# Local and global attention with a gated MLP on one core: a new order table, wishes for engines, displaced TensorE operations, and another conversion of the float64 weights

## The chip, the cores and the metric

The kernel runs on one core of a Trainium2 chip. The metric is the device time of one execution in microseconds (us). Engines are named as in the profile: PE (TensorE; PEld is its weight load), DVE (VectorE), ACT (ScalarE), POOL (GpSimd), SP (SyncE, which issues the DMAs).

## What is computed

```python
# attention: B, H, S, D = 4, 8, 768, 64; n_global 8, n_local 96
scores = q @ k.T / sqrt(D) + bias        # bias: slope of the head times distance
scores = where(is_global | is_local, scores, -1e9)
a = exp(scores - max); a = a / (sum(a) + 1e-9)
x = (a @ v) as (B, 768, 512)
# gated MLP: w_in (512, 1024) and w_out (512, 512) are float64, w_sg (768, 768) is float32
h = gelu(x @ w_in); u, v = h[..., :512], h[..., 512:]
v_n = (v - mean(v)) / sqrt(var(v) + 1e-6) * g_ln
v_s = einsum('ts,bsd->btd', w_sg, v_n) + b_sg
out = x + (u * v_s) @ w_out
```

## The kernel before

**Attention.** There are 48 units: four batches, three stretches of 256 queries, four pairs of heads. A unit is two DMAs (qk, v); `score`, PE products of 64x64 quarters of the array (`s_ps`, L886); `softmax`, in which DVE adds the bias and takes the row minimum (L918), ACT takes the exponential (L923), a small operation adds 1e-9 to the sums (L930 ACT, L932 POOL, L934 DVE), DVE takes the reciprocal (L936) and one of ACT (L943), POOL (L945) or DVE (L948) scales the rows; `turn`, which turns the weights over, by PE transposes (L1007) and copies (L1012, L1013) for the first 16 units and by DVE transposes (L974) and a DMA through memory later; `weigh`, the quarter products with v (`av`, L1035); and `take`, which puts the result into x as a high and a low part (`xh` L1132 or L1133, high L1144 or L1146, low L1150). A run of quarter products between products of the full array is called a block below.

**MLP.** Every product is three PE matmuls (L539, L540, L541: high by high and the two mixed ones). The tiles are V (`mm_ps<-win,x`, 512 columns, with gelu L558 to L563 and the layer norm: statistics L597 to L599 on DVE, a power on POOL L602, the normalising L604 on DVE, and the split in high L573 and low L577), U (`mm_ps<-x,win`, 384 columns), the mix over the sequence (`mm_ps<-wsg,z`, L631, L634 and a split) and the output (`mm_ps<-gt,wout`, L662, L665, DMA L668).

**Weights.** `load_split` brings 20 float64 pieces (16 of 256 columns, 4 of 512: `win` and `wout`) as pairs of int32 words. ACT scales the upper word (L704); three DVE passes, a shift (L707) and two with two inputs (L709, L711), put the lost bits in; then a high part (L714 ACT, L715 DVE) and a low part (L716) are split off. The pieces of `wsg` need the split only.

**What sets the order.** `Plan` records 2566 operations, each with one or more ways (an engine and an estimate of its cost). `due` gives every operation a due time from the order of the PE operations; `search` adds to it a shift from the table `SHIFTS` (one digit for each operation, in steps of 0.05 us) as its `key`; `order` goes through the engines and picks, among the operations that are ready, the one with the lowest key and the way that would end first; `emit` chains the instructions of an engine in that order. In the first 75 us `keep_on` (L483 to L489) puts matmuls with zeros (`<-on`, "fillers" below) ahead of a PE operation where the plan has PE idle. In the start the first 12 units, the pieces of `win` and the first V tiles are worked off together; the first U tile follows after 20 V and attention steps, then the mix tiles, and the first output tile at about 86 us.

## Time and profile before

| what | value |
|---|---|
| median of three runs | 410.22 us (410.19 to 410.34) |
| span of the profiled execution | 410.0 us |
| PE busy | 398.2 us (97%) |
| DVE busy | 322.0 us (79%) |
| ACT busy | 216.7 us (53%) |
| POOL busy | 183.6 us (45%) |
| clock of PE, 12 to 30 us | 0.92 |

The span is the time from the first to the last instruction of the one execution that the hardware profiler recorded; no separate time is given for that execution. An engine that is busy for nearly all of a stretch can set the pace there; what an engine waited for is told by its row in the view of waits. Matmuls are pipelined, so the time between two starts, not the duration of one, is what a matmul costs.

### The profile page before, as it was taken

What the parts mean: (1) busy time and instruction counts of PE and PEld (TensorE: products, weight loads), DVE (VectorE), ACT (ScalarE), POOL (GpSimd) and SP (SyncE); (2) the same over time, 40 slices, a digit from 0 to 9 for tenths busy, and PEclk for the clock granted to TensorE, in tenths of its full rate; (3) what the DMA queues carried; (4) which work ended last, traced back from release to release, by engine and by line L of the source; (5) the groups of instructions that cost most, each with busy time, mean ns of one, the idle gap of its engine ahead of it and who ended that gap; (6) DMA issues with size and microseconds to landing.
All of it is one profiled execution on the core that took longest, in us unless ns stands there. A gap on an engine that the chain in (4) does not pass through costs nothing.

```text
span 410.0 us, 12434 instructions
## 1 busy us (share of the span) xinstructions
PE 398.2 (97%) x4593; PEld 362.0 (88%) x4593; DVE 322.0 (79%) x1088; ACT 216.7 (53%) x726; POOL 183.6 (45%) x332
## 2 busy tenths in 40 slices
PE   7999999999999999999999999999999999999993
PEld 4768778898998989899999888999999889999993
DVE  7998999999978999877677899867677668663552
ACT  5999999875646856535432666551432325310110
POOL 3324553373548675666446454563446242303100
PEclk9899999999999999999999999999999999999998
DMA  7874765237786896646888673652856410001002
GB/s 232 283 228 121 218 199 160 81 106 234 229 237 213 264 289 197 174 148 200 254 228 248 217 235 96 203 153 96 245 186 203 148 39 21 0 2 70 10 1 83
DMA packets 50035, 67.14 MB, mean 164 GB/s; under 512 B 5808, under 2 KB 33968, under 8 KB 49968
## 3 DMA queue, kind: packets, MB, share of 16 engines
q1 hardware_dynamic: 49968, 66.28, 52.7%
q8 instruction: 38, 0.62, 0.6%
q14 instruction: 29, 0.24, 0.2%
HBM read 47.91 MB, written 18.35 MB: 162 GB/s over the span
## 4 chain that ended last, share of the span: by engine, by line
PE 85%; DVE 9%; ACT 1%; issue 1%; POOL 0%; DVEq 0%; POOLq 0%
PE mm_ps L539 24%; PE mm_ps L541 23%; PE mm_ps L540 23%; PE av L1035 7%; PE s_ps L886 6%; PE tps L1007 2%; DVE p L918 1%; DVE stage L711 1%; DVE stage L709 1%; DVE st L597 1%; DVE win L716 1%; DVE vg L563 1%; DVE stage L707 0%; DVE p L948 0%; DVE vg L560 0%
## 5 line engine op out<-in xcount | busy, mean ns | idle before, releaser
L923 ACT ACTIVATE p<-p,pst 128x168 f32<-128x168 f32 (+1 forms) x192 | 80.9, 424 | 28.8 <-DVE pst L918 23.7
L945 POOL TENSOR_SCALAR p<-p,pst 128x168 f32<-128x168 f32 (+1 forms) x137 | 56.8, 430 | 27.5 <-DVE pst L936 27.0
L539 PE MATMUL mm_ps<-wsg,z 128*128 128x384 f32 x192 | 65.0, 339 | 0.0
L541 PE MATMUL mm_ps<-wsg,z 128*128 128x384 f32 x192 | 64.3, 335 | 0.1
L540 PE MATMUL mm_ps<-wsg,z 128*128 128x384 f32 x192 | 64.2, 334 | 0.0
L918 DVE CUSTOM_DVE_ANT_0 p<-s_ps,bias 128x168 f32<-128x168 f32 (+1 forms) x192 | 53.5, 319 | 6.5 <-PE s_ps L886 4.9
L665 POOL TENSOR_TENSOR o<-o,x 128x384 f32<-128x384 f32 x28 | 28.6, 1021 | 52.5 <-DVE o L662 39.0
L1035 PE MATMUL av<-pt,v 64*64 64x128 f32 (+1 forms) x1408 | 48.8, 252 | 1.0 <-DVE pt L1013 0.7
L1035 PEld LDWEIGHTS av<-pt,v 64*64 64x64 f32 x1408 | 37.4, 134 | 9.9 <-issue 5.3
L539 PE MATMUL mm_ps<-x,win 128*128 128x384 f32 x128 | 43.9, 343 | 0.0
L539 PE MATMUL mm_ps<-gt,wout 128*128 128x384 f32 x128 | 43.0, 336 | 0.0
L540 PE MATMUL mm_ps<-gt,wout 128*128 128x384 f32 x128 | 43.0, 336 | 0.0
L541 PE MATMUL mm_ps<-gt,wout 128*128 128x384 f32 x128 | 42.9, 335 | 0.0
L541 PE MATMUL mm_ps<-x,win 128*128 128x384 f32 x128 | 42.8, 335 | 0.0
L540 PE MATMUL mm_ps<-x,win 128*128 128x384 f32 x128 | 42.8, 334 | 0.0
L558 ACT ACTIVATE u<-mm_ps 128x384 f32<-128x384 f32 x32 | 15.6, 488 | 45.7 <-PE mm_ps L541 45.0
L886 PE MATMUL s_ps<-qk 64*64 64x64 f32 (+2 forms) x1408 | 39.5, 242 | 0.1
L539 PE MATMUL mm_ps<-win,x 128*128 128x512 f32 x96 | 39.5, 411 | 0.0
L886 PEld LDWEIGHTS s_ps<-qk 64*64 64x64 f32 x1408 | 34.2, 135 | 4.1 <-issue 2.7
L541 PE MATMUL mm_ps<-win,x 128*128 128x512 f32 x96 | 37.7, 393 | 0.0
L540 PE MATMUL mm_ps<-win,x 128*128 128x512 f32 x96 | 37.7, 392 | 0.0
L539 PEld LDWEIGHTS mm_ps<-wsg,z 128*128 128x128 f32 x192 | 36.0, 188 | 1.4 <-issue 0.9
(112 smaller groups left out, 902.1 us busy)
## 6 DMA issues: line engine op xcount, KB each, us to landing
qk<-in_qk_in_dram SPq DMA_DIRECT2D x32, 328.0 KB, 3.8
pt<-far SPq DMA_DIRECT2D x24, 384.0 KB, 4.9
v<-in_v_in_dram SPq DMA_DIRECT2D x32, 256.0 KB, 4.1
out_dram<-o SPq DMA_DIRECT2D x32, 192.0 KB, 3.4
far<-tt SPq DMA_DIRECT2D x48, 96.0 KB, 1.9
far<-stage SPq DMA_DIRECT2D x48, 96.0 KB, 2.4
qk<-in_qk_in_dram SPq DMA_DIRECT2D x16, 276.0 KB, 3.6
v<-in_v_in_dram SPq DMA_DIRECT2D x16, 192.0 KB, 4.2
```

The lines of the kernel that those rows point to most:

```text
L539: mm(ps.ap, ah, bh, start=(i == 0), stop=False)
L540: mm(ps.ap, ah, bl, start=False, stop=False)
L541: mm(ps.ap, al, bh, start=False, stop=(i == n - 1))
L558: op([on_act(n) + (lambda: nc.scalar.activation(out.ap, h.ap, AF.Square, scale=math.sqrt(GELU_C * GELU_A)),)], [h], [out])
L563: op([on_dve(n) + (lambda: nc.vector.scalar_tensor_tensor(out.ap, out.ap, 1.0, h.ap, ALU.add, ALU.mult),)], [h], [out])
L665: lo = lambda eng: eng.tensor_tensor(o.ap, o.ap, xm[:, 1, :].bitcast(F32), ALU.add)
L886: nc.tensor.matmul(s_ps[h][e * HQ:(e + 1) * HQ, i * W + c0:i * W + c0 + n], qk[rows, qc:qc + HQ], qk[rows, QW + k0:QW + k0 + n], start=Tru ...
L918: nc.vector.tensor_tensor_reduce(out=p[:, g, cols], in0=s_ps[h][:, i * W:i * W + nk], in1=bias[:, 2 * j + h, w0:w0 + nk], op0=ALU.add, op1 ...
L923: op([on_act(nk, 0.225) + (lambda p=p, g=g, cols=cols, i=i: nc.scalar.activation(p[:, g, cols], p[:, g, cols], AF.Exp, bias=st[:, 0, i, g: ...
L945: op([on_pool_ts(nk, -0.10) + (partial(scaled, lambda o, a, c: nc.gpsimd.tensor_scalar(o, a, c, 1.0, ALU.mult, ALU.mult)),), on_act(nk, 0. ...
L1007: nc.tensor.transpose(tps[:, a * P:(a + 1) * P], pc[:, c:c + P], ident)
L1035: nc.tensor.matmul(to, v[rows, vc:vc + D], of, stop=True, skip_group_check=True, **kw)
```

## The change

There is a new `SHIFTS` table, whose digits now run over the whole range. For a PE operation a digit no longer shifts its due time: it displaces the operation by so many places in the list of PE operations. A second table, `WAYS`, has a letter for each operation: A, D or P allow only the way on ACT, DVE or POOL, a dash allows all. POOL is added as a way for the high parts (`split`, `load_split`, `take`) and the bias, ACT and POOL as ways of the normalising; for this POOL makes two small operations instead of one after the statistics (`power`). In the conversion of float64 the passes L707, L709 and L711 give way to a copy of one 16-bit quarter beside another (`beside`, on POOL or DVE), a DVE shift with a mask on the upper words, and one DVE pass with two inputs.

```diff
--- before.py
+++ after.py
@@ -11,6 +11,7 @@
 F32 = mybir.dt.float32
 F32R = mybir.dt.float32r
 BF16 = mybir.dt.bfloat16
+I16 = mybir.dt.int16
 I32 = mybir.dt.int32
 AF = mybir.ActivationFunctionType
 ALU = mybir.AluOpType
@@ -58,30 +59,57 @@
 DIGITS = "0123456789ABCDEFGHIJKLMNOPQRSTUVWXYZabcdefghijklmnopqrstuvwxyz-"
 
 SHIFTS = (
-    "VdcVXYiVeZpLWbTXPWjkIXjPCbojUQ-XVe7ZLXXrICVYZVKMNTFBePnQ8WNYfaeuV2PlWAhAQRISUVFT3qSMPPWYPLUvdWapCJTaXfAYUTgl"
...
+    "XHB003VbY000E5QRmULOkerH3KLhj-nH8w8d5z6L70v5P50Z5nt2x99CbT62UGEO7nA-p7cCGM0pttPmt-00gfuL3JHH5T0K20bCPcGL039W"
...
+)
+
+WAYS = (
+    "------A------------ADD--PD---------D-ADDP-DD--A-A--------P--PAP---DA----DD--A-A-----------P-P--P--------D--D"
...
 )
 
 TURNS = 16
@@ -278,9 +306,12 @@
             for other in o.before:
                 other.after.append(o)
             o.left = len(o.before)
-            if o.quarters is not None:
-                t += self.switch(mode, o.quarters)
-                o.due, t, mode = t, t + o.ways[0][1], o.quarters
+        pe = [o for o in self.ops if o.quarters is not None]
+        places = {o: i + o.moved for i, o in enumerate(pe)}
+        self.pe = sorted(pe, key=places.get)
+        for o in pe:
+            t += self.switch(mode, o.quarters)
+            o.due, t, mode = t, t + o.ways[0][1], o.quarters
         later = {}
         for kind, bufs in kinds.items():
             for b, next_b in zip(bufs, bufs[self.places[kind]:]):
@@ -298,8 +329,8 @@
 
     def search(self, start):
 
-        for o, digit in zip(self.ops, SHIFTS, strict=True):
-            o.key = o.due + (DIGITS.index(digit) - 31) * 0.05
+        for o in self.ops:
+            o.key = o.due + (0.0 if o.quarters is not None else o.moved * 0.05)
         done, end = self.order(start, RULES)
         assert end < math.inf, "no op can go on"
         return done
@@ -341,7 +372,7 @@
-        pe = [o for o in self.ops if o.quarters is not None]
+        pe = self.pe
...
-            for w in o.ways:
+            for w in o.open:
                 wait[w[0]].append(o)
...
@@ -493,6 +524,9 @@
         bb = nc.cur_bb.bb
         why, sync = (mybir.DependencyInfo(c, mybir.DependencyReason.DATA)
                      for c in (mybir.DependencyClass.NoSync, mybir.DependencyClass.Sync))
+        for o, digit, way in zip(self.ops, SHIFTS, WAYS, strict=True):
+            o.moved = DIGITS.index(digit) - 31
+            o.open = [w for w in o.ways if w[0][0] == way] or o.ways
         self.due()
         for o in self.search(start):
             n = len(bb.instructions)
@@ -573,7 +607,8 @@
             put(out[:, 0, :], src.ap)
 
         op([on_act(n, 0.03) + (partial(high, nc.scalar.copy),),
-            on_dve_ts(n / 2) + (partial(high, nc.vector.tensor_copy),)], [src], [(out, 0)])
+            on_dve_ts(n / 2) + (partial(high, nc.vector.tensor_copy),),
+            on_pool_ts(n) + (partial(high, nc.gpsimd.tensor_copy),)], [src], [(out, 0)])
         lo = lambda eng: eng.tensor_tensor(out[:, 1, :], src.ap, out[:, 0, :].bitcast(F32),
                                            ALU.subtract)
         op([on_dve_sb(n) + (lambda: lo(nc.vector),), on_pool(n) + (lambda: lo(nc.gpsimd),)],
@@ -599,10 +634,18 @@
             nc.vector.tensor_scalar(rs[:, 0:1], mv[:, 1:2], 4e-6, None, ALU.add)
 
         op([on_dve(FF, 0.40) + (stats,)], [g], [st, mv, rs])
-        op([("POOL_TS", 0.55, 0.6, lambda: nc.gpsimd.tensor_tensor(
-            rs[:, 1:2], rs[:, 0:1], w.mhalf, ALU.pow))], [], [rs])
+
+        def power():
+            nc.gpsimd.tensor_tensor(rs[:, 1:2], rs[:, 0:1], w.mhalf, ALU.pow)
+            nc.gpsimd.tensor_scalar(rs[:, 0:1], mv[:, 0:1], rs[:, 1:2], -1.0, ALU.mult, ALU.mult)
+
+        op([("POOL_TS", 0.80, 0.85, power)], [mv], [rs])
         op([on_dve_ts(FF, -0.14) + (lambda: nc.vector.tensor_scalar(
-            g.ap, g.ap, mv[:, 0:1], rs[:, 1:2], ALU.subtract, ALU.mult),)], [mv, rs], [g])
+            g.ap, g.ap, mv[:, 0:1], rs[:, 1:2], ALU.subtract, ALU.mult),),
+            on_act(FF, 0.05) + (lambda: nc.scalar.activation(
+                g.ap, g.ap, AF.Identity, bias=rs[:, 0:1], scale=rs[:, 1:2]),),
+            on_pool_ts(FF) + (lambda: nc.gpsimd.tensor_scalar(
+                g.ap, g.ap, mv[:, 0:1], rs[:, 1:2], ALU.subtract, ALU.mult),)], [mv, rs], [g])
         z = self.z[t] = Buf(lambda i: self.zp.tile([P, 2, FF], F32R, tag=f"z{i}", name="z"), "z")
         self.split(g, z, FF)
 
@@ -704,15 +747,19 @@
         op([on_act(n, 0.07) + (lambda: nc.scalar.mul(
             f.ap, words()[:, :, 1].bitcast(F32), 2.0 ** -112),)], [raw], [f])
 
-        op([("DVE_TS", 0.07 + n / 1850, 0.15 + n / 1850, lambda: nc.vector.tensor_scalar(
-            a(), a(), 3, None, ALU.logical_shift_left))], [], [f])
+        def beside(put):
+            of = raw.ap.bitcast(I16).rearrange("p (n w) -> p n w", w=4)
+            put(of[:, :, 2], of[:, :, 1])
+
+        op([on_pool_ts(n) + (partial(beside, nc.gpsimd.tensor_copy),),
+            on_dve_ts(n) + (partial(beside, nc.vector.tensor_copy),)], [f], [raw])
+        op([on_dve_ts(n) + (lambda: nc.vector.tensor_scalar(
+            words()[:, :, 1], words()[:, :, 1], 13, -0x7ffffff9, ALU.arith_shift_right, ALU.bitwise_and),)], [], [raw])
         op([on_dve_sb(n, 0.02) + (lambda: nc.vector.scalar_tensor_tensor(
-            a(), words()[:, :, 0], 29, a(), ALU.logical_shift_right, ALU.bitwise_or),)], [raw], [f])
-        op([on_dve_sb(n, 0.02) + (lambda: nc.vector.scalar_tensor_tensor(
-            a(), words()[:, :, 1], -0x80000000, a(), ALU.bitwise_and, ALU.bitwise_or),)],
-           [raw], [f])
+            a(), a(), 3, words()[:, :, 1], ALU.logical_shift_left, ALU.bitwise_or),)], [raw], [f])
     op([on_act(n, 0.03) + (lambda: nc.scalar.copy(t[:, 0, k, cols], f.ap),),
-        on_dve_ts(n / 2) + (lambda: nc.vector.tensor_copy(t[:, 0, k, cols], f.ap),)], [f], [(t, part)])
+        on_dve_ts(n / 2) + (lambda: nc.vector.tensor_copy(t[:, 0, k, cols], f.ap),),
+        on_pool_ts(n) + (lambda: nc.gpsimd.tensor_copy(t[:, 0, k, cols], f.ap),)], [f], [(t, part)])
     lo = lambda eng: eng.tensor_tensor(t[:, 1, k, cols], f.ap, t[:, 0, k, cols].bitcast(F32),
                                        ALU.subtract)
     op([on_pool(n) + (lambda: lo(nc.gpsimd),), on_dve_sb(n) + (lambda: lo(nc.vector),)],
@@ -856,7 +903,9 @@
                 op([("DVE_TS", 0.065 + n / 3300, 0.145 + n / 3300, lambda h=h, cols=cols: nc.vector.tensor_scalar(
                     bias[:, h, cols], dist[:, cols], -(2.0 ** (2 - h)), None, ALU.mult)),
                     on_act(n) + (lambda h=h, cols=cols: nc.scalar.mul(
-                        bias[:, h, cols], dist[:, cols], -(2.0 ** (2 - h))),)],
+                        bias[:, h, cols], dist[:, cols], -(2.0 ** (2 - h))),),
+                    on_pool_ts(n) + (lambda h=h, cols=cols: nc.gpsimd.tensor_scalar(
+                        bias[:, h, cols], dist[:, cols], -(2.0 ** (2 - h)), 1.0, ALU.mult, ALU.mult),)],
                    [(dist_b, part) for part in parts], [(bias_b, (h, part)) for part in parts])
 
     def wire(words):
@@ -1144,6 +1193,8 @@
             op([on_act(t1 - t0, 0.03) + (lambda x=x, cols=cols, src=src: nc.scalar.copy(
                 x[:, 0, cols], half[:, src]),),
                 on_dve_ts((t1 - t0) / 2) + (lambda x=x, cols=cols, src=src: nc.vector.tensor_copy(
+                    x[:, 0, cols], half[:, src]),),
+                on_pool_ts(t1 - t0) + (lambda x=x, cols=cols, src=src: nc.gpsimd.tensor_copy(
                     x[:, 0, cols], half[:, src]),)], [half], ts)
 
             def low(eng, x=x, cols=cols, src=src):
```

Counted over the program, PE has 41 blocks of quarter products instead of 45, all its other products unchanged in number, and 83 fillers instead of 57. The scaling of rows stands on DVE in 53 operations (19 before), on ACT in 56 (36) and on POOL in 83 (137); of the 24 normalisings 9 are on DVE, 10 on ACT and 5 on POOL; of the 20 copies `beside`, 13 are on DVE (3 of them of 512 columns) and 7 on POOL. Ahead of the first U tile stand 20 quarter products more than before, in 18 blocks (19 before); between the first U and the first output tile there are 2 blocks (5), and behind it 21 (21).

PE at the first U tile (`av` are products with v, `s_ps` scores, `on` fillers), before:

```order
L541 MATMUL mm_ps<-win,x 128x512
L1035 MATMUL av<-pt,v 64x128 x4
L1035 MATMUL av<-pt,v 64x64 x4
L539 MATMUL mm_ps<-x,win 128x384
L540 MATMUL mm_ps<-x,win 128x384
```

And after the change, where eleven more pairs like the last two rows stand before the first U product:

```order
L575 MATMUL mm_ps<-win,x 128x512
L1084 MATMUL av<-pt,v 64x128 x4
L1084 MATMUL av<-pt,v 64x64 x4
L935 MATMUL s_ps<-qk 64x104 x4
L935 MATMUL s_ps<-qk 64x64 x4
L935 MATMUL s_ps<-qk 64x104 x4
L935 MATMUL s_ps<-qk 64x64 x4
L1084 MATMUL av<-pt,v 64x128 x4
L519 LDWEIGHTS on
L519 MATMUL mm_ps<-on 128x384
```

A score and part of a further product with v have moved ahead of the first U tile, and twelve fillers of 384 columns stand there where there were none.

DVE at the conversions of the last pieces of `win` ahead of the first U tile, before:

```order
L709 SCALAR_TENSOR_TENSOR stage<-stage 128x256
L707 TENSOR_SCALAR stage<-stage 128x256
L711 SCALAR_TENSOR_TENSOR stage<-stage 128x256 x3
L709 SCALAR_TENSOR_TENSOR stage<-stage 128x256
L716 TENSOR_TENSOR win<-stage,win 128x256
L711 SCALAR_TENSOR_TENSOR stage<-stage 128x256
L716 TENSOR_TENSOR win<-stage,win 128x256
L715 CAST win<-stage 128x256
```

And after:

```order
L756 TENSOR_SCALAR stage<-stage 128x256
L758 SCALAR_TENSOR_TENSOR stage<-stage 128x256 x2
L756 TENSOR_SCALAR stage<-stage 128x256 x2
L758 SCALAR_TENSOR_TENSOR stage<-stage 128x256 x2
L763 TENSOR_TENSOR win<-stage,win 128x256 x4
L763 TENSOR_TENSOR wsg<-stage,wsg 128x384
```

Each piece has two passes here in place of three, and the copies `beside` stand further ahead; four low parts of `win` follow one another.

POOL at the first V tiles, before:

```order
L945 TENSOR_SCALAR p<-p,pst 128x168
L602 TENSOR_TENSOR rs<-rs,small 128x1
L1150 TENSOR_TENSOR x<-xh,x 128x128 x2
L945 TENSOR_SCALAR p<-p,pst 128x168
L577 TENSOR_TENSOR z<-vg,z 128x512
L932 TENSOR_SCALAR pst<-pst 128x4
```

And after:

```order
L607 CAST z<-vg 128x512
L994 TENSOR_SCALAR p<-p,pst 128x168
L612 TENSOR_TENSOR z<-vg,z 128x512
L639 TENSOR_TENSOR rs<-rs,small 128x1
L640 TENSOR_SCALAR rs<-mv,rs 128x1
L647 TENSOR_SCALAR vg<-vg,mv,rs 128x512
L607 CAST z<-vg 128x512
L612 TENSOR_TENSOR z<-vg,z 128x512
```

POOL now has high parts and a normalising of 512 columns among its work, and the second small operation behind the power.

## Rows read from the trace of the kernel before

**Rows 1.** The page: the span, and the busy time of each engine.

```profile
span 410.0 us, 12434 instructions
PE 398.2 (97%) x4593; PEld 362.0 (88%) x4593; DVE 322.0 (79%) x1088; ACT 216.7 (53%) x726; POOL 183.6 (45%) x332
```

**Rows 2.** Windows: length, then PE, PEld, DVE, ACT, POOL busy, PE clock, DMA share, GB/s.

```profile
12.00:30.00 18.00, 17.21 (x323) 13.15 (x317) 17.83 (x70) 17.41 (x68) 6.14 (x11) 0.92 0.75 248
30.00:60.00 30.00, 29.25 (x568) 22.71 (x568) 27.50 (x128) 29.57 (x110) 15.30 (x31) 1.00 0.62 190
60.00:86.00 26.00, 25.43 (x229) 22.37 (x229) 25.69 (x84) 23.32 (x76) 10.76 (x15) 1.00 0.39 114
86.00:403.50 317.50, 317.40 (x3365) 298.49 (x3363) 241.42 (x761) 138.63 (x449) 147.60 (x249) 1.00 0.52 159
```

**Rows 3.** PE's waits from 62 to 404 us: total, times, longest.

```profile
PE tps L1007 <- DVE vg L563: 0.5, 1, 0.5
```

**Rows 4.** Timeline at the first U tile: start, duration, engine, operation.

```profile
66.34 0.67 PE L1035 MATMUL av<-pt,v 64*64 64x128 f32 x16
66.51 0.83 DVE L716 TENSOR_TENSOR win<-stage,win 128x256 fp32r<-128x256 f32 x2
66.69 0.80 POOL L945 TENSOR_SCALAR p<-p,pst 128x128 f32<-128x128 f32 x1
66.94 0.44 PE L539 MATMUL mm_ps<-x,win 128*128 128x384 f32 x1
```

**Rows 5.** Timeline of PE: a switch inside a block, then a block between full products.

```profile
304.35 1.08 PE L1035 MATMUL av<-pt,v 64*64 64x128 f32 x48
305.25 0.77 PE L886 MATMUL s_ps<-qk 64*64 64x104 f32 x32
...
315.51 0.33 PE L540 MATMUL mm_ps<-wsg,z 128*128 128x384 f32 x1
315.69 0.34 PE L541 MATMUL mm_ps<-wsg,z 128*128 128x384 f32 x1
315.96 1.13 PE L1035 MATMUL av<-pt,v 64*64 64x128 f32 x48
317.02 0.50 PE L539 MATMUL mm_ps<-win,x 128*128 128x512 f32 x1
317.36 0.40 PE L540 MATMUL mm_ps<-win,x 128*128 128x512 f32 x1
317.59 0.39 PE L541 MATMUL mm_ps<-win,x 128*128 128x512 f32 x1
```

**Rows 6.** DVE groups by form, float64 passes: count, busy us, mean ns, idle before.

```profile
L709 DVE SCALAR_TENSOR_TENSOR stage<-stage 128x256 int32<-128x256 int32 x16 | 6.9, 431 | 0.2
L707 DVE TENSOR_SCALAR stage<-stage 128x256 int32<-128x256 int32 x16 | 4.9, 305 | 0.0
...
L709 DVE SCALAR_TENSOR_TENSOR stage<-stage 128x512 int32<-128x512 int32 x4 | 2.8, 693 | 0.1
...
L707 DVE TENSOR_SCALAR stage<-stage 128x512 int32<-128x512 int32 x4 | 1.7, 436 | 0.0
```

**Rows 7.** DVE groups by form, of kinds that change engine.

```profile
L604 DVE TENSOR_SCALAR vg<-vg,mv,rs 128x512 f32<-128x512 f32 x24 | 12.9, 541 | 1.8 <-POOL rs L602 1.6
...
L948 DVE TENSOR_SCALAR p<-p,pst 128x168 f32<-128x168 f32 x16 | 6.0, 398 | 0.1
...
L1133 DVE COPY xh<-av 128x128 f32<-128x128 f32 x11 | 3.1, 277 | 0.0
...
L716 DVE TENSOR_TENSOR win<-stage,win 128x512 fp32r<-128x512 f32 x4 | 2.7, 681 | 0.0
...
L1150 DVE TENSOR_TENSOR x<-xh,x 128x256 fp32r<-128x256 f32 x4 | 1.7, 414 | 0.0
```

**Rows 8.** Scaling on DVE: duration in ns least/median/longest, first and last start, forms.

```profile
L948 DVE TENSOR_SCALAR p<-p,pst x19: 277/341/1076, 9.0 to 133.2; 128x168 f32<-128x168 f32 x16, 128x128 f32<-128x128 f32 x3
```

**Rows 9.** The same of scaling on POOL.

```profile
L945 POOL TENSOR_SCALAR p<-p,pst x137: 361/405/811, 9.0 to 312.6; 128x168 f32<-128x168 f32 x111, 128x128 f32<-128x128 f32 x26
```

More of the change, by code (lines that the diff above doesn't have):

```diff
@@ new lines @@
+    "kQVEMxTUafgesQvKso9Fcqm-u8xN-m-2A0lCv--0m-Sxu0W7Jjf8CXTHjz6g-ZXX5YHbh8E2FEjL1HsS3BSRuaAnzWx-yN-H835Prbsd6HMQ"
+    "8FYComk9Xd-E0p01h2M-O5czBMTXEB-K00bMBrH-RYPswDuSbSP7N8qANKPJ--SOiQhf60bVqf9kkqGLDOrvPHkuOi-BtOvJgwpSHBhq50ZV"
+    "egqc1l-cuqHOxnO64GrCEOR00Xgpk7NX8USB5E09Za-6tPbgdO6Th0vUmPrW0Ua-d0L0Sv0xL-8usvg7H0"
+)
+WAYS = (
+    "------A------------ADD--PD---------D-ADDP-DD--A-A--------P--PAP---DA----DD--A-A-----------P-P--P--------D--D"
+    "-----A-------------------AD------DA---A----------P-A-PA--D--AP------D-A-------------D-ADAD--D--DP--------D--"
+    "APDDP---D--------P-P--P--D--A-------P-DA-PDD-A-A--------P-DPPA--P------------DP-------DADPPP---A--------A-DA"
+    "D-------D--------DDP-DP---D-----------D-D--P---------------------A--D-D-A--------A-ADDA-----PD--P--PD------P"
+    "---A--A-A--------A-P-DD------P------D---------D---------D-------------D-DPPA--D--P--------D-D--A------------"
+    "D--P-AP--------A------A---PP--------------APAA-DD-AD--P--D--PD--D--A------------AD------------D-------------"
+    "--P--A-----A--------D-PAP----------D--PD--D---P--P--D-------------PDD---------------PAD--------APP---A------"
+    "--P---AP--P--PD--D---P-----D----------------D--------P-----------D-ADDP-----------AP--A-----PD-PP-----------"
+    "P-------------D------P---------A---------------A--APP------------------------DA-D---------P-P-PA--P-P-------"
+    "---------------AD-PP---------P-A--A---D-P--------------------------A--A--D---------P-PPD-----------DAAD----D"
+    "AD--------D------------------A-D---------D-PDDP----------AAAA-----------A------D-----------P----------------"
+    "--------A-------------D-P-PD--------P-AAAP-----------DD-----D-----------DAP-----------------------A-A-A-----"
+    "----D--P-D--------D---P------------A------------A------------------------DPP----------------DD--------------"
+    "--A-D-A---------P-AAPD----------DDAP--------------DD--------DAP---------------------------P-----------------"
+    "--------A-A---------A-PDPA--------P---PA----------------AP---------------------------A-D-A-----------DADP---"
+    "-----P-PDAD---DPD---------------DD--------PP----------------A---A---------A-DAA---------D-DPPD----------DD--"
+    "----P-----------DPP-----D--------------------A---------A--PDP-----------D------------DPD-----P-----------AA-"
+    "--------------------------A---------A-A-D---------D-D-PD----------P-D------------------------------------P--"
+    "----------------P-------------------D-----------D--AA---------P---A----------------D--------D-P-------------"
+    "D-------------P------P------------------D-D---------D-A-------------P-DD----------------DD------------------"
+    "------------D---------D--DP---------D-D-PD----PP----------------PD--------D------------D-D-A-----------AA---"
+    "---D-----------D-------P--P---D-----------ADP-----D------------AD-----P-----------D------------DA-----------"
+    "-------------P-P---------------D-P---------------DDP-------PA--------------D-------------P------D-----------"
+    "-----PDP----------------DP---------------DDP-------DDD---D-D----------------P-----"
@@ L398, in order @@
                         continue
-                    way = next(w for w in o.ways if w[0] == e)
+                    way = next(w for w in o.open if w[0] == e)
                     if begin(way) > t + 0.1:
@@ L404, in order @@
                     lag = {w[0]: (PATIENCE if calm and w[0] != "POOL" else 0.0)
-                           + (price if w[0] == "DVE" else 0.0) for w in o.ways}
+                           + (price if w[0] == "DVE" else 0.0) for w in o.open}
                     if any(max(begin(w), t) + w[2] + lag[w[0]] < t + way[2] + lag[e]
-                           for w in o.ways):
+                           for w in o.open):
                         continue
@@ L413, in order @@
                 o.begin, o.way, o.since = max(t, begin(way)), way, free[e]
-                for w in o.ways:
+                for w in o.open:
                     wait[w[0]].remove(o)
```

43 lines of the change are left out of this document (20 added, 23 removed).

## The prediction

> **What bounds the kernel now.** I read the page first. The span is 410.0 us, and PE is busy for 97% of it, DVE for 79%, the others for about half [rows 1]. PE is therefore the engine whose row to follow; the question is where its missing 3% are, and what a PE matmul costs beyond its products.
>
> The windows by stage come next [rows 2]. Behind 86 us PE is busy 317.40 of 317.50 us: nothing that another engine does there can shorten the run, only PE's own work can. Between 12 and 60 us DVE is busy 45.3 of 48.0 us and ACT 47.0 of 48.0; PE reads as busy too, but part of that is fillers, and the stretch is paced by DVE and ACT. From 60 to 86 us PE has 0.57 us idle and DVE 0.31: either can be the bound. The view of PE's waits from 62 us on says the same in one line: a single wait of 0.5 us [rows 3].
>
> At the first U tile the timeline shows who ended last. PE issued its first U product at 66.94, and the DVE row of two low parts of `win` began at 66.51 and took 0.83 for both, so the first ended at about 66.92 [rows 4]. DVE's conversion of weights released PE there.
>
> Last, the price of going between quarter products and full ones [rows 5]. Inside a block, 48 products take 305.25 - 304.35 = 0.90. Between full products, entering takes 315.96 - 315.69 = 0.27 where a full product takes 315.69 - 315.51 = 0.18 (+0.09); the same 48 take 317.02 - 315.96 = 1.06 (+0.16); and the first full product behind takes 0.34 where the next takes 0.23 (+0.11). A block costs 0.36 us on PE.
>
> **The change, part by part.** The baseline is the profiled execution, 410.0 us; the median of the runs, 410.22, lies 0.2 above, and I add the gain to the median. 0.2% of it, about what a measurement of this kernel can tell from no change, is 0.8 us.
>
> 1. *Fewer blocks on PE.* One block fewer ahead of the first U tile, three fewer between it and the first output tile, none fewer behind. The three are worth 3 x 0.36 = 1.1 us if PE paces 60 to 86 us, and nothing if DVE does. The one ahead lies in a stretch that DVE and ACT pace: nothing, with PE's waits as the cover.
>
> 2. *PE work moved ahead of the first U tile.* 20 quarter products, at 0.90/48 = 0.019 each, make 0.4 us. They fill PE while it waits for `win`, and are gone behind it: 0.4 on the path if PE paces what follows, otherwise nothing.
>
> 3. *The conversion.* Ahead of the first U tile DVE converts 4 pieces of 512 columns and 8 of 256 in part. Before, it runs there 4 + 4 shifts (L707) and 8 + 8 passes with two inputs: 4 x 0.436 + 4 x 0.305 + 8 x 0.693 + 8 x 0.431 = 12.0 us [rows 6]. After, it runs 4 + 4 passes with two inputs, 4 + 4 of the new shifts, and 3 + 2 of the copies `beside`. The new shift and the copy read every second word, or every fourth half word, which no single-input row shows. One bound is L707, contiguous, 0.436 and 0.305; the other L709, which reads the same every second word, 0.693 and 0.431. I take L709, the row with the same access: (4 + 4 + 3) x 0.693 + (4 + 4 + 2) x 0.431 = 11.9 us. A pass less has become a copy on the same engine: 0.1 us. By L707 it is 7 x 0.436 + 6 x 0.305 + 4 x 0.693 + 4 x 0.431 = 9.4 us, or 2.6 less.
>
> 4. *Other DVE work ahead of the first U tile.* 15 operations leave DVE, two normalisings at 0.541 and two low parts at 0.681 among them, and 17 come, six copies `xh` at 0.277 and three low parts of x at 0.414 among them [rows 7]. With the means of the rest from the same view the sum is -0.4. With step 3: DVE -0.5 ahead of the first U tile, which is on the path, since DVE released PE there [rows 4]. Counted on to the first output tile, the same sum is -0.3: later DVE work takes half of it back.
>
> 5. *Fillers.* Twelve of 384 columns stand ahead of the first U tile, 12 x 0.18 = 2.1 us by the spacing of a 384-column product [rows 5]. While PE waits for DVE they cost nothing; if `win` is there earlier than planned, up to 2.1 us on PE. I take 0.
>
> 6. *The second small operation on POOL*, 24 times. Its bound is POOL's fastest scaling, 0.361 [rows 9], below it nothing. In the trace DVE's normalising waited 1.6 us in all for the power [rows 7]; with three tiles' powers ahead of the first U tile, up to 1.1 us. Those waits are covered by other DVE work, and 15 of the 24 normalisings have left DVE: 0.
>
> 7. *Scaling* moves from POOL (54 fewer) to DVE (34 more) and ACT (20 more), nearly all behind 86 us. DVE pays 34 x 0.398 = 13.5 us there [rows 7] and has 317.5 - 241.4 = 76 us free [rows 2]; nothing waits for it on PE. The cost is 0, up to the 0.5 us of one longer wait. The end, from the last matmul to the last DMA, has the same operations.
>
> The sum: the large end, PE pacing from the first U tile on, is -0.5 - 0.4 - 1.1 = -2.0. The small end, DVE pacing up to the first output tile, is -0.3. In 60 to 86 us both have little idle time, and the fillers of step 5 lean to the small side; I take -1.4, a little nearer the large end because PE's waits there sum to only 0.5 us. 410.2 - 1.4 = **408.8 us**.
>
> **The rivals.**
>
> *Strided passes run as fast as contiguous ones.* Step 3's other bound: DVE is 2.6 us lighter ahead of the first U tile. For it: L707 needs 0.131 us for 256 more columns (0.436 - 0.305), half of what L709 needs (0.262), and L707 has one input where L709 has two. Against it: no strided single-input row, and ACT, 1.0 us idle in 12 to 60 us, has as much work ahead of the first U tile as before. So 1.0 of the 2.6 can count at once: 408.8 - 1.0 = 407.8; with ACT not in the way 406.2. I put it at 407.2. The Trainium skill (VectorE: DVE Perf Modes, What auto-detection actually checks) gives both read ports to an operation with one source in SBUF whatever its step, as long as the outer dimension is even; by that rule this rival is the forecast. The trace agrees for contiguous words only, with the 0.131 us above.
>
> *No change.* DVE paces up to the first output tile, the three blocks lie in PE's waits, and the fillers fill what was gained: -0.3 to 0, 410.0 us. For it: DVE is busy 25.69 of 26.00 us from 60 to 86 [rows 2], and its sum to that tile is the same within 0.3.
>
> *Slower: POOL and DVE hold each other up.* Ahead of the first output tile POOL gets some 24 operations of kinds that it did not have there: copies, high parts of x, z and weights, low parts of 512 columns, a normalising. In the trace a POOL scaling that began beside DVE's two-input row took 0.80 [rows 4], against a median of 0.405 [rows 9]; the other way round, DVE's scaling takes 0.398 on the mean of 168 columns and 0.277 at the least [rows 7, 8], with 1.076 as the longest. If each new POOL operation holds DVE up by that mean excess, 0.12, the start grows by 24 x 0.12 = 2.9 us: 408.8 + 2.9 = 411.7. It decides from 2.2 us of hold-up, or 0.09 for each. The Trainium skill (SBUF — State Buffer, Who interferes with whom) says that a VectorE operation with two SBUF inputs and a GpSimd one that reads SBUF exclude each other, and that the one issued first holds the other up for its whole length. The 0.80 us fits it; by it alone a POOL operation of 1 us could cost DVE as much. Against it: POOL is a third to half busy there [rows 2], and it can be POOL that waits.
>
> **How the numbers follow.** Forecast 0.40, strided passes fast 0.20, no change 0.24, slower 0.16. The forecast's own range, 408.0 to 410.0, is the two ends of the sum, with 0.2 more at the large one. Faster than 409.4: most of the forecast (0.36) and the first rival, 0.56. Slower than 411.0: 0.16. Between them 0.28. For 8 in 10 the range takes in the first rival down to 406.6 and the no-change case whole, and reaches 411.2 into the slow one.
>
> **What would show it.** Right: the first U product starts about 1 us earlier than 66.94, the first output tile 1 to 2 us earlier, and PE from there on takes the same time. Step 1 is right if PE has about 41 blocks with the price above. Step 3 is right if the new shift takes about 0.43 at 256 columns, and wrong (first rival) at about 0.30. The slow rival shows as DVE scaling or copies with means over 0.5 in 12 to 86 us and a first U product later than 67. The prediction is wrong if PE's waits behind 86 us grow past 1 us: then the moved scaling or the normalising on ACT is late, and step 7 has failed.

## The result, and the profile after

The change takes 413.45 us (411.89 to 413.81, five executions) where before takes 410.22 (410.15 to 410.41): a ratio of 1.0065 [1.0047, 1.0082]. It is slower by 3.2 us, outside the range of the forecast and above all three rivals' times.

In each of these executions the time is the span and 1.8 us more. The execution behind [rows 1] had a span of 410.0 and so took about 411.8, above its median. An execution of before unchanged beside the experiments had a span of 408.6; it is the one that traces are compared with below, as the control.

The page of the profile after: span and busy times, answering to [rows 1].

```profile
span 411.6 us, 12513 instructions
PE 399.1 (97%) x4619; PEld 362.9 (88%) x4619; DVE 331.8 (81%) x1131; ACT 224.3 (54%) x736; POOL 178.7 (43%) x303
```

The same windows as [rows 2] (length, then PE, PEld, DVE, ACT, POOL busy, PE clock, DMA share, GB/s), of the change.

```profile
12.00:30.00 18.00, 17.06 (x362) 13.68 (x356) 17.26 (x72) 17.96 (x68) 10.63 (x17) 1.00 0.76 239
30.00:60.00 30.00, 29.47 (x568) 23.01 (x566) 27.64 (x129) 29.28 (x107) 19.28 (x36) 1.00 0.64 197
60.00:86.00 26.00, 25.84 (x238) 22.84 (x236) 25.78 (x83) 23.03 (x72) 15.91 (x24) 1.00 0.43 137
86.00:405.00 319.00, 316.96 (x3353) 297.35 (x3353) 252.18 (x802) 146.40 (x470) 126.86 (x199) 1.00 0.52 157
```

From 30 to 86 us PE is as busy as before or busier. Behind 86 us it was idle for 317.50 - 317.40 = 0.1 us; now it is for 319.00 - 316.96 = 2.04. PE's longest waits there, of the change (waiting tile and line, what ended the wait, total, times, longest):

```profile
PE s_ps L935 <- DMA qk<-in_qk_in_dram: 0.6, 1, 0.6
PE mm_ps L573 <- DVE pst L967: 0.4, 1, 0.4
PE av L1084 <- DMA pt<-far: 0.4, 1, 0.4
PE av L1084 <- issue: 0.3, 1, 0.3
PE s_ps L935 <- DVE pst L967: 0.3, 1, 0.3
```

The timeline of PE gives the two landmarks used from here on, the first product of the first output tile ("first O") and the last matmul. Of the control:

```profile
98.13 0.33 PE L539 MATMUL mm_ps<-gt,wout 128*128 128x384 f32 x1
...
402.96 0.34 PE L541 MATMUL mm_ps<-gt,wout 128*128 128x384 f32 x1
```

Of the change:

```profile
96.84 0.33 PE L573 MATMUL mm_ps<-gt,wout 128*128 128x384 f32 x1
...
405.82 0.34 PE L575 MATMUL mm_ps<-gt,wout 128*128 128x384 f32 x1
```

The start became 98.13 - 96.84 = 1.3 us shorter. The stretch from first O to the last matmul, called **the rest** below, went from 304.83 to 308.98: 4.2 longer. The table has these for each run (V is the start of the first V product, U that of the first U product; V, U, first O and the rest are of the one profiled execution; the time and the ratio are of all its executions against before on the same chip).

| run | median us | ratio and interval | V | U | first O | the rest |
|---|---|---|---|---|---|---|
| before | 410.22 | | 29.28 | 66.94 | 98.33 | 304.73 |
| control (c0) | 411.13 | 1.0012 [1.0001, 1.0022] | 29.08 | 66.72 | 98.13 | 304.83 |
| the change | 413.45 | 1.0065 [1.0047, 1.0082] | 28.79 | 67.69 | 96.84 | 308.98 |
| e1 no fillers | 413.51 | 1.0063 [1.0047, 1.0079] | 31.02 | 69.09 | 99.39 | 307.01 |
| e6 start | 413.03 | 1.0060 [1.0044, 1.0076] | 29.92 | 67.31 | 97.98 | 307.56 |
| e2 scaling to POOL | 413.82 | 1.0075 [1.0049, 1.0101] | 28.85 | 67.77 | 96.93 | 309.40 |
| e7 tail | 412.21 | 1.0042 [1.0024, 1.0060] | 30.13 | 69.05 | 98.37 | 307.10 |
| e4 conversion, DVE | 411.13 | 1.0016 [1.0000, 1.0031] | 29.25 | 66.90 | 98.22 | 305.43 |
| e5 conversion, POOL | 415.10 | 1.0110 [1.0094, 1.0126] | 30.48 | 68.27 | 101.59 | 305.99 |
| e8 old conversion | 414.03 | 1.0082 [1.0051, 1.0113] | 29.19 | 68.00 | 97.59 | 306.74 |
| e9 repaired | 413.04 | 1.0051 [1.0032, 1.0071] | 29.19 | 67.10 | 97.55 | 305.99 |
| e3 old tail | 413.48 | 1.0075 [1.0053, 1.0097] | 28.84 | 67.76 | 97.12 | 307.19 |
| e10 wishes off | 422.99 | 1.0314 [1.0279, 1.0350] | 29.38 | 68.31 | 97.65 | 317.52 |
| e11 no displacement | 420.59 | 1.0233 [1.0200, 1.0265] | 31.14 | 71.16 | 104.72 | 308.65 |
| e12 more fillers | 412.59 | 1.0052 [1.0031, 1.0073] | 28.87 | 67.79 | 96.99 | 307.07 |
| e13 fewer fillers | 414.49 | 1.0080 [1.0061, 1.0099] | 29.83 | 68.73 | 98.05 | 310.30 |
| e14 tail and fillers | 411.75 | 1.0015 [1.0002, 1.0029] | 29.80 | 68.70 | 98.04 | 305.95 |
| e15 held clock | 411.17 | 1.0016 [1.0002, 1.0029] | 28.92 | 67.87 | 97.01 | 306.70 |

The control differs from itself by up to 0.2%, so a ratio below about 1.002 is no difference.

Two things have to be kept in mind with the table. From V to first O the change and every run that starts from it, e11 apart, need 68.05 to 68.40 us, where before, the control and e4 need 68.97 to 69.05; what differs more in the start lies ahead of V. And a profile is one execution: those of e9 and e12 were the fastest of their runs, those of e1 and e13 the slowest. Behind first O the change, e1, e6, e12 and e13 run the same list of operations, and their rests are 308.98, 307.01, 307.56, 307.07 and 310.30 (e13's with half the clock from 122 to 125 us). A rest that differs by no more than this is not told apart by one profile.

### The profile page after: what moved, and what is told of

Read it like the earlier page. It is cut to its first block, busy times and chain, and to the rows that moved or that the text cites. A ratio compares the mean times of both kernels' runs of the same rounds, so it can differ in the third digit from the quotient of the medians.

```text
span 411.6 us, 12513 instructions
## 1 busy us (share of the span) xinstructions
PE 399.1 (97%) x4619; PEld 362.9 (88%) x4619; DVE 331.8 (81%) x1131; ACT 224.3 (54%) x736; POOL 178.7 (43%) x303
## 4 chain that ended last, share of the span: by engine, by line
PE 71%; DVE 12%; ACT 7%; DMA 4%; issue 2%; SPq 1%; POOL 1%; DVEq 0%; POOLq 0%; ACTq 0%
PE mm_ps L573 20%; PE mm_ps L574 20%; PE mm_ps L575 20%; PE av L1084 6%; PE s_ps L935 5%; ACT p L972 3%; DMA qk<-in_qk_in_dram 3%; DVE p L967 2%; DMA far<-stage 1%; ACT pt L1061 1%; PE s_ps L519 1%; PE tps L1056 1%; DVE st L632 1%; ACT p L992 1%; DVE vg L594 1%
## 5 line engine op out<-in xcount | busy, mean ns | idle before, releaser
L994 POOL TENSOR_SCALAR p<-p,pst 128x168 f32<-128x168 f32 (+1 forms) x83 | 38.8, 478 | 42.6 <-DVE pst L985 36.1
L972 ACT ACTIVATION_READ_ACCUMULATOR p<-p,pst 128x1 f32 x192 | 36.9, 192 | 0.0
```

The costliest lines, as they stand in the source:

```text
L972: op([on_act(nk, 0.225) + (lambda p=p, g=g, cols=cols, i=i: nc.scalar.activation(p[:, g, cols], p[:, g, cols], AF.Exp, bias=st[:, 0, i, g: ...
L994: op([on_pool_ts(nk, -0.10) + (partial(scaled, lambda o, a, c: nc.gpsimd.tensor_scalar(o, a, c, 1.0, ALU.mult, ALU.mult)),), on_act(nk, 0. ...
```

## The experiments

Where a run starts from the change, its list of operations was kept as the change has it, and only what the diff names differs; e3, e10 and e11 let the planner choose anew.

**The control.** No edit.

> The kernel before, unchanged, as a control, to have the span and granted clock of each of its runs. 410.2 us (0.2 either side). If the profile shown ahead of the prediction was of an execution with a low clock at the start (0.92 from 12 to 30 us), these spans are about 1.7 us shorter than 410.0; if not, they are 410.

Its profiled execution has the span of 408.6 that is used above.

**The start: the twelve fillers.** In the change they ran ahead of the first U product. The timeline there (start, duration, engine, operation), of the change:

```profile
65.38 0.81 ACT L645 ACTIVATE vg<-vg,rs 128x512 f32<-128x512 f32 x1
65.47 1.94 DVE L763 TENSOR_TENSOR win<-stage,win 128x256 fp32r<-128x256 f32 x4
65.83 2.16 PE L519 MATMUL mm_ps<-on 128*128 128x384 bf16 x12
66.09 0.70 ACT L760 CAST win<-stage 128x256 fp32r<-128x256 f32 x2
67.69 0.47 PE L573 MATMUL mm_ps<-x,win 128*128 128x384 f32 x1
```

Either the fillers hold U up, or `win` is late and they fill the wait. e1 leaves them out:

```diff
-        for _ in range(self.zeros(o)):
+        for _ in range(0 if o.begin > 60.0 else self.zeros(o)):
```

> The change with the plan untouched, without the twelve fillers ahead of the first U tile. Theory A (the fillers hold PE up there: they ran from 65.83 to 67.69 while the first low part of win was done at about 66.0): 1.7 us faster than the change, 411.7. Rival (PE waits for the weights there anyway): no difference, 413.4.

Measured: no gain in the time. PE waits in their place. The same timeline of e1, where the bracket is the wait and what ended it (V lies 2.2 us later here; see the clock below):

```profile
67.61 0.83 ACT L645 ACTIVATE vg<-vg,rs 128x512 f32<-128x512 f32 x1
68.33 0.71 ACT L760 CAST win<-stage 128x256 fp32r<-128x256 f32 x2
69.09 0.44 PE L573 MATMUL mm_ps<-x,win 128*128 128x384 f32 x1 [0.94 <-ACT win L760]
...
73.46 0.56 PE L1056 MATMUL tps<-ident,p 128*128 128x128 f32 x3 [0.71 <-ACT p L992]
...
76.06 0.44 PE L1056 MATMUL tps<-ident,p 128*128 128x128 f32 x2 [0.47 <-DVE p L997]
```

Both theories hold in part. In the change the last high parts of `win` were done at 66.79, and U came behind the fillers at 67.69; from V to U it needs 38.90, and e1 needs 38.07. So the fillers did hold U up, by 0.8 us. But e1 has three waits, 2.1 us in all, where the change has 1.9 us of fillers and none of these waits, and from V to first O the two need 68.05 and 68.37: nothing of the 0.8 is left there.

A normalising that the change gave to ACT stands ahead of the last high parts of `win`. e6 moves it behind two of them, without the fillers:

```diff
+    done = [o for o in done if o.number != 555]         # the normalising on ACT
+    done.insert(done.index(of[244]) + 1, of[555])       # behind this high part
```

> The change without the twelve fillers, and with the normalising on ACT that stands ahead of the last two high parts of win moved behind them; nothing else. Theory D (that normalising of 0.81 us held the first U product up by 0.9 us once the fillers were gone): the first U product at 66.4 to 66.9 where no low clock falls in the start, against 67.7; the whole 0.5 to 1.2 us faster than the change. Rival (the next late thing, a scaling ahead of the transposes of unit 14, takes it back): U early, and the same place at 90 us of PE work as the change.

U starts 0.4 earlier than in the change, 1.5 if counted from V, and the ratio is the same within its interval. The next waits take over behind U (0.68 and 0.72 us at 68.6 and 72.4), and from V to first O it needs 68.06. Up to first O the fillers cost nothing; what they cover is a chain of late operations.

**The rest: scaling and loads.** e2 gives POOL back the 34 scalings that DVE got behind 90 us:

```diff
+    for o in done:
+        if o.begin > 90.0 and [w[0] for w in o.ways] == ["POOL", "ACT", "DVE"] and o.way[0] == "DVE":
+            o.way = o.ways[0]
```

> The change with the same order, but the 34 scalings behind 90 us that the table of wishes puts on DVE are on POOL again. Theory B (the added DVE work there makes DVE late in reading score banks and turning weights over, and PE waits): 2 to 2.5 us faster than the change, 411.2, and the PE waits behind 100 us down from 4.5 to about 2 us. Rival C (the order itself, DMAs and displaced PE work, makes PE wait): 413.4 within 0.5, or slower.

The waits for DVE at 216 to 256 us are gone, but the rest of its profile is no shorter: a load of queries and keys is later still. The longest wait of e2 there:

```profile
PE s_ps L935 <- DMA qk<-in_qk_in_dram: 1.9, 1, 1.9
```

The timeline of the change shows what that load stands behind (SPq is SP's queue):

```profile
117.54 1.83 SPq L1031 DMA_DIRECT2D far<-stage  x4
119.42 0.46 SPq L918 DMA_DIRECT2D qk<-in_qk_in_dram  x1
...
124.52 0.82 PE L935 MATMUL s_ps<-qk 64*64 64x104 f32 x32 [0.58 <-DMA qk<-in_qk_in_dram]
```

And of the control:

```profile
117.92 0.43 SPq L869 DMA_DIRECT2D qk<-in_qk_in_dram  x1
120.03 1.80 SPq L982 DMA_DIRECT2D far<-stage  x4
```

Before, the load went out ahead of the four stores; now it stands behind them, and it takes SP 1.8 us to issue them. (DVE writes what they store, but the view shows no wait of SP for DVE at this place.) e7 puts it ahead again, gives two late high parts of `wsg` to ACT, and returns the scalings behind 190 us to POOL:

```diff
+    done = [o for o in done if o.number != 978]         # the load of qk
+    done.insert(done.index(of[936]), of[978])           # ahead of the stores
...
+        if o.number in (848, 851):                      # high parts of wsg
+            o.way = o.ways[0]
```

> The change with three edits behind 100 us: one qk load is issued ahead of the stores of turned weights that it waited behind at 117 us, two high parts of wsg are on ACT again, and the scalings behind 190 us that the wishes put on DVE are on POOL. Theory (these three waits make up most of the 3.3 us that PE waits behind 100 us): the waits at 117 to 125 us and at 216, 241 and 256 us are gone, and the whole is 2 to 3 us faster than the change, 410.5 to 411.5. Rival (other transfers and reads come late in their place): PE's waits behind 100 us stay above 2 us.

In its profile all waits named above are gone, and two for `wsg` are left, 0.4 and 0.2 us. The rest is 308.98 - 307.10 = 1.9 shorter, but that alone shows nothing: e1, without these edits, has 307.01, and there PE did not wait for the load, though it stands behind the stores as in the change. Lines of e1:

```profile
119.41 1.80 SPq L1031 DMA_DIRECT2D far<-stage  x4
121.25 0.47 SPq L918 DMA_DIRECT2D qk<-in_qk_in_dram  x1
...
124.88 1.55 PE L935 MATMUL s_ps<-qk 64*64 64x104 f32 x64
```

So with the same order PE waits for the load in some profiles and not in others. The median of e7 is 1.2 below that of the change, and the intervals of the two ratios overlap. In its profiled execution the start was 1.5 longer (first O 98.37), which leads to the clock.

**The conversion.** e4 and e5 put the new one into before, in its order, with all copies `beside` on DVE or on POOL; e8 puts the three old passes into the change.

```diff
+        op([("DVE_TS", 0.07 + n / 1850, 0.15 + n / 1850, partial(beside, nc.vector.tensor_copy))], [f], [raw])   # e5: nc.gpsimd
```

> The kernel before with its own order, but the new conversion of the float64 weights, all 20 copies beside on DVE. By the means in the trace of the change (copy 0.54 and 0.81, new shift 0.33 and 0.51, two-input pass 0.43 and 0.71) DVE has 28.5 us of conversion instead of 25.6. Theory (DVE paces the start, and the copy is dearer than the pass that it replaces): 1.5 to 3 us slower than before. Rival (the start has room on DVE): no difference within 0.8.

> The same with all 20 copies on POOL: DVE's conversion falls from 25.6 to about 17 us, POOL gets 18 us more ahead of 105 us. Theory (DVE paces the start): 2 to 4 us faster than before, 407 to 408.5. Rival (POOL and DVE hold each other up, or POOL's copy of 0.8 us is late for the shift that follows it on DVE): no faster than before.

> The change with its order, but with the three DVE passes of the kernel before as the conversion, all on DVE; seven copies leave POOL. Theory (the copy beside is dear: 0.54 and 0.81 us on DVE, 0.82 and 1.33 on POOL, and nothing is won by it): 0.5 to 1 us faster than the change, about 412.7. Rival (the seven copies on POOL relieve DVE): slower than the change.

With the copies on DVE the time is that of before; with all on POOL, first O is 3.4 us later. In the profile of the change with the old passes the start is 0.3 (U) to 0.8 us (first O) longer, and the ratio is no better. The groups of DVE by form in the change give the prices, answering to [rows 6]:

```profile
L756 DVE TENSOR_SCALAR stage<-stage 128x256 int32<-128x256 int32 x16 | 5.1, 327 | 0.0
L752 DVE COPY stage<-stage 128x256 int16<-128x256 int16 x10 | 5.0, 541 | 0.0
...
L752 DVE COPY stage<-stage 128x512 int16<-128x512 int16 x3 | 2.3, 813 | 0.0
...
L756 DVE TENSOR_SCALAR stage<-stage 128x512 int32<-128x512 int32 x4 | 1.9, 506 | 0.0
```

The new shift takes 0.327 and 0.506, nearer L707 than L709; the copy takes 0.541 and 0.813, more than either.

e9 joins e7's edits, the old conversion and the start without its twelve fillers, and loads two pieces of `wsg` earlier:

```diff
+    for o, at in ((978, 936), (847, 935), (850, 893)):  # 847, 850: loads of wsg
```

> All repairs together: the edits of the run with three repairs behind 100 us, the old conversion, no fillers ahead of the first U tile, and two loads of wsg issued earlier on SP, ahead of the stores and loads of turned weights that they waited behind. Theory (the late loads, bank reads and the conversion are the loss, and the rest of the change is worth the 0.8 us by which it led at 90 us of PE work): PE's waits behind 100 us under 1 us, 409.5 to 411. Rival (every repair uncovers the next wait): 412 or more.

In its profile the rest is 305.99, and the view names no wait of PE behind 100 us. That execution was the fastest of seven; its ratio, 1.0051, has an interval that overlaps the change's.

**The tables one by one.** e3 uses the new tables only for operations below 900 (the old shifts, no wishes and no displacement behind); e10 drops the wishes from operation 640 on; e11 drops the displacement.

```diff
+            if o.number >= TAIL:                               # e3: TAIL is 900
+                o.moved, o.open = 0, o.ways                    # and the old shifts
...
+            o.open = [w for w in o.ways if w[0][0] == way and o.number < 640] or o.ways   # e10
+            o.moved = 0 if o.quarters is not None else DIGITS.index(digit) - 31           # e11
```

> The new tables for operations up to number 899, which is about the first output tile; behind it the old shifts, no wishes and no displacement. Theory (the start of the change gains 1.8 us at 90 us, and what is lost comes from the tables behind it): 408.5 to 409, faster than the kernel before. Rival (the loss behind 90 us comes from the start, late weights or buffers, or from the granted clock): above 411.

> The change without wishes for engines for operations from number 640 on (behind the first U tile); the plan chooses its engines there, which also makes 46 blocks of quarter products out of 41. Theory (the wishes put work where it makes PE wait): PE's waits of more than 0.2 us behind 100 us sum to under 1.5 us instead of 3.1, five blocks more cost 1.8 us, 413 in all. Rival (the order, not the engines): the waits stay, 415.

> The change with its tables, but no PE operation displaced: 48 blocks instead of 41. By the price of 0.36 us the seven blocks cost 2.5 us, of which about two lie behind the first U tile's start: 415 to 416 if nothing else changes. Rival (the displaced order is what makes loads late): waits behind 100 us fall, 412 to 413.

In e3 PE is idle for 0.5 us of the rest, and the rest is still 2.4 longer than the control's: its trace has 24 blocks of quarter products there where the control and the change have 21, and three at 0.36 [rows 5] are 1.1; about 0.8 is left. e10 has 26 blocks there and 6.5 us of idle PE; e11 has 27, and a start that is 8 us longer. These runs do not price one table, since the planner chose all else anew; e10 and e11 show that the change without its wishes, or without its displacement, is slower by 2% and more.

**The clock at the start.** Profiles differed in the start by up to 2 us. Windows from 10 us on (columns as above), of the execution of before behind [rows 1]:

```profile
10.00:12.00 2.00, 1.32 (x30) 1.08 (x33) 1.84 (x12) 2.00 (x9) 0.00 (x0) 0.84 1.00 340
12.00:14.00 2.00, 2.00 (x34) 1.55 (x28) 2.00 (x6) 2.00 (x12) 0.78 (x1) 0.50 0.62 248
```

The second of them in the control:

```profile
12.00:14.00 2.00, 1.32 (x25) 0.72 (x17) 2.00 (x6) 2.00 (x12) 0.78 (x1) 1.00 0.78 299
```

Both of e7:

```profile
10.00:12.00 2.00, 0.98 (x11) 0.51 (x12) 1.23 (x11) 1.98 (x9) 1.57 (x2) 0.92 0.97 315
12.00:14.00 2.00, 2.00 (x48) 1.86 (x44) 1.55 (x6) 1.70 (x9) 0.34 (x2) 0.50 0.68 272
```

And the second in the change:

```profile
12.00:14.00 2.00, 2.00 (x56) 1.76 (x49) 2.00 (x7) 2.00 (x12) 0.35 (x2) 1.00 0.69 277
```

Before and e7 run at half clock (1.2 GHz) from 12 to 14 us, after a stretch in which PE was idle for part; the control and the change are at full clock. The control had the same idle time from 10 to 12 us (PE busy 1.32), and so had the change (0.99), so the idle time alone does not make the clock fall. In the control PE is busy from 12 to 14 us for only 1.32 of 2 us, and half the clock delays the kernel before only a little: V starts at 29.28 in place of 29.08, 0.2 later. In the change PE is busy throughout, fillers among it, and e7, whose edits all lie behind 90 us, starts V at 30.13 in place of 28.79, 1.3 later; e6 and e1, at half clock too, at 29.92 and 31.02 (in e1 it is half from 12 to 16 us). e12 adds six fillers to the first transposes, e13 leaves out the 53 between 12 and 30 us:

```diff
+        for _ in range(self.zeros(o) + 6 * (o.number == 47)):                  # e12
+        for _ in range(0 if 11.5 < o.begin < 30.0 else self.zeros(o)):         # e13
```

> The change with six more fillers of 384 columns ahead of the first transposes, in the 1.5 us in which PE is idle at 8 to 9.7 us; nothing else. Theory E (PE's idle time there is followed by half clock at 11 to 17 us, and the new start passes it on): mean clocks of 0.997 and more in most runs, and the median 1 us or more below the change, 412 or less, with a smaller spread. Rival (the low clock does not depend on it): clocks of 0.990 to 0.996 as before, no gain.

> The change without the 53 fillers that stand between 12 and 30 us. Theory F (these fillers are run whatever is late, so that a delay by low clock at 12 to 17 us is not taken up by PE's waits): where the clock falls at 12 us, no more than 0.5 us of it is left at 30 us, and the median is about 412. Rival (without them the clock falls later or longer): more time at half clock, 414 or more.

e13 is no faster: the fillers do not sit on the path there. Its profiled execution has the clock at 0.62 and 0.53 from 12 to 14 and 14 to 16 us, and V at 29.83, 1.0 later than the change at full clock, so leaving the fillers out does not take up what half the clock costs. Its executions have mean clocks of 0.985 to 0.995, e12's 0.988 to 1.0, and e12's ratio overlaps that of the change: the six fillers did not hold the clock in every execution, and no gain from them is shown. (A mean clock holds the end too: in the profile of the change the clock is 0.61 from 408 us on, behind the last matmul.) e14 joins e7's tail, the two earlier `wsg` loads and e12's fillers; e15 adds ten more:

```diff
+        for _ in range(self.zeros(o) + {47: 8, 45: 2, 65: 6}.get(o.number, 0)):   # e15
```

> The change with its conversion, the three repairs behind 100 us, the two earlier loads of wsg, and the six more fillers at 8 us. If late loads and low clock are the whole loss, 409.5 to 410.5, level with the kernel before or below it; if each repair uncovers the next wait, 411.5 or more.

> The kernel with three repairs behind 100 us and two earlier loads of wsg, with 16 more fillers at three places between 8 and 12 us instead of six at one. If the low clock after PE's idle time at 8 to 12 us is the remainder: clocks of 0.997 and more in most runs, 409.5 to 410.5, level with the kernel before or 0.2% below it. Rival (the clock falls all the same, or the fillers are in the way): 411.5 or more.

e14 stands at 1.0015 of before in place of 1.0065, level with the control. It differs from e12 by the edits behind 90 us alone and ran beside it, twelve executions of each: 411.75 against 412.59, and the two ratios, 1.0015 and 1.0052, have intervals that do not touch. So these edits together are worth about 0.8 us by the medians. e9 has them too and stands at 1.0051, with the old conversion; the run beside it that has the old conversion without them, e8, stands at 1.0082. The profiled execution of e14 is at half clock for most of 12 to 14 us (0.55) in spite of the fillers; its rest is 305.95, and its only wait named behind 100 us is this, of the view of waits of e14:

```profile
PE s_ps L935 <- DMA qk<-in_qk_in_dram: 0.2, 1, 0.2
```

e15 holds the clock (0.996 to 0.999 in all executions, e14's mean is 0.995) but the ratio is e14's: holding it longer than e14 does is worth nothing that these runs can tell. No version is faster than before.

## Why the prediction was wrong

**Steps 1 and 2 were right in their sum.** First O was forecast 1 to 2 us earlier and came 1.3 earlier (1.5 against the execution of [rows 4]). 1.0 of it lies between V and first O and is there in every run that starts from the change, e11 apart; the other 0.3 lies ahead of V and turns into a loss at half clock. No run tells the three blocks of step 1 and the moved products of step 2 apart.

**Step 3 was half right.** The shift came out near the cheaper bound and the copy beyond the dearer one: with them the sum of step 3 is 4 x 0.506 + 4 x 0.327 + 3 x 0.813 + 2 x 0.541 + 4 x 0.693 + 4 x 0.431 = 11.3 us, where 11.9 was forecast. The Trainium skill (VectorE: DVE Perf Modes, What auto-detection actually checks) gives both read ports to an operation with one source in SBUF and sets no condition on its step beside an even outer dimension. The trace nearly agrees for the shift (0.327 beside 0.305) and not for the copy of every fourth half word (0.541). On the time the conversion with its copies as they stand, or all on DVE, had no effect that can be measured (e8, e4); with all on POOL it was slower (e5).

**Steps 4 and 5 failed at the first U product.** The forecast had DVE release PE there, as in [rows 4], so U about 1 us earlier; U came at 67.69, 0.75 later. The fillers released it: step 5 put them at nothing, and they held U up by 0.8 (from V 38.90 with them, 38.07 in e1). Without them ACT releases it: the normalising that became ACT's, 0.81 us, stands ahead of two high parts of `win` (e1's 0.94). At first O step 5's price of 0 held, but for another reason than that DVE is late: e1 and e6 removed the fillers, e6 the normalising too, and the next waits took over. (12 x 0.18 is 2.2, not 2.1; the twelve took 1.9.)

**Step 6 was not tested.** The normalising on ACT waited 2.9 us in all for POOL's second small operation, L640; no run tells whether that reached PE. The group in the change:

```profile
L645 ACT ACTIVATE vg<-vg,rs 128x512 f32<-128x512 f32 x10 | 8.1, 811 | 3.1 <-POOL rs L640 2.9
```

**Step 7 failed, and it decided the sign.** "Nothing waits for it on PE" was argued from busy shares: 76 us free on DVE. PE was idle 2.04 us behind 86 us in place of 0.10, which the forecast had named as what would prove it wrong. But only part is the moved scaling (e2 removes those waits and gains nothing). The other part had no term at all in the sum: the order of SP's queue, where a load now stands behind four stores, and high parts of `wsg` that are late. That these edits, e7's three and the two earlier loads of `wsg`, together bring time back is shown by e14 beside e12 (1.0015 and 1.0052); how much each does is not. The rest is 308.98 in the profile of the change, 307.01 to 310.30 in the profiles of others with the same list behind first O, and 305.95 to 306.70 in those of e9, e14 and e15, which have all of these edits; PE's longest wait behind 100 us differs with it (1.8 us in e13, 1.0 in e12, 0.3 in e1). Of the 1.1 us by which e14's rest is still longer than the control's, about half stands at its one wait: the block of 120 quarter products at 156.9 us takes 3.70 from the last full product ahead of it to the second behind it, where the control's block of the same products takes 3.15. The other half stays open.

**The baseline was too long.** The sum stood on an execution of before that took about 1.6 us more than the median; 1.3 of it lay behind the last matmul (410.0 - 403.06 = 6.9 us to the end, 408.6 - 402.96 = 5.6 in the control) and 0.2 in the start at half clock. The forecast's stages were not touched by it. What it had no term for is the clock: half the clock from 12 us on costs the change's start 1.0 to 1.3 us (V at 29.80 to 30.13 in e6, e7, e13 and e14, against 28.79). It is not what set the profiled execution apart: its span, 411.6, is 1.5 above the fastest of the change, 410.1, and its clock is 1.00 in all its windows from 12 to 405 us. What sets the executions of the change apart is not shown; the waits behind first O differ from profile to profile, and may do it.

**The rivals.** Strided passes: half right, and without effect on the time. No change: wrong. POOL and DVE holding each other up: the sign was right and the mechanism not. POOL's scaling takes 0.478 on the mean where it took 0.430, DVE's 0.360 where it took 0.398 [rows 7], and the start is shorter, not longer. The groups by form, of POOL before, then of POOL and DVE in the change:

```profile
L945 POOL TENSOR_SCALAR p<-p,pst 128x168 f32<-128x168 f32 x111 | 46.3, 430 | 17.3 <-DVE pst L936 16.9
...
L994 POOL TENSOR_SCALAR p<-p,pst 128x168 f32<-128x168 f32 x70 | 32.8, 478 | 38.3 <-DVE pst L985 32.5 <-ACT p L972 5.0 <-ACT pt L1061 0.4
...
L997 DVE TENSOR_SCALAR p<-p,pst 128x168 f32<-128x168 f32 x44 | 14.8, 360 | 0.4
```

## What to carry to other kernels

Where PE is busy to 0.1 us over 317, any move on another engine can only open waits, so price every moved operation by who waits for it at its place, not by the free time of the engine that gets it; and follow the loads in SP's queue past the stores that they now stand behind. Expect a removed wait to show the next one: here three in a row from the first U product on. Compare a change with several executions of the kernel before, since one trace can be 1.6 us off its median; and before an edit is credited with a shorter stretch, look for a run that lacks the edit and has the stretch as short, as e1 does beside e7. What settled it was a pair that ran side by side and differed by the edits alone, e12 and e14.

## What the runs showed of the hardware

A copy of every fourth half word took 0.541 us for 256 columns on DVE and 0.815 on POOL, where DVE's pass over words with two inputs took 0.431 [rows 6]. A normalising of 128x512 took 0.541 on DVE [rows 7], 0.811 on ACT and 2.108 on POOL; the groups of POOL by form in the change:

```profile
L647 POOL TENSOR_SCALAR vg<-vg,mv,rs 128x512 f32<-128x512 f32 x5 | 10.5, 2108 | 0.0
...
L752 POOL COPY stage<-stage 128x256 int16<-128x256 int16 x6 | 4.9, 815 | 0.3 <-DVE z L612 0.3
```

Half the clock from about 12 us on put V 0.2 us later in before and 1.0 to 1.3 later in the change's order (e6, e7, e13, e14). Why the price differs is not shown: e13 has no fillers in that stretch and pays 1.0 all the same.
